# VectorE's product of rank and class ahead of the next step's first mask, in a kernel of linear attention and two feed-forward layers

## The chip, the core and the metric

The kernel runs on one core of a Trainium2 chip. The metric is the device time of one execution in microseconds (us). The kernel before took 776.17 us in the median of three runs.

## The reference

Three layers follow each other. The first is a linear attention with a decaying state, for 4 sequences, 8 heads, 768 positions and 48 channels:

```python
for t in range(S):
    cur = np.einsum('bhd,bhe->bhde', u[None] * kt, vt)
    y[:, :, t] = np.einsum('bhd,bhde->bhe', rt, state + cur)
    state = wt[:, :, :, None] * state + np.einsum('bhd,bhe->bhde', kt, vt)
```

The second sends each of the 3072 tokens (384 numbers each) to one of 8 experts, if its skip score is above zero; the third is a dense layer of 2048 inner channels:

```python
do_compute = x @ w_skip > 0
logits = xc @ w_gate
e_idx = np.argmax(logits, axis=1)
gate_w = probs[np.arange(len(xc)), e_idx]          # softmax of the logits
y[mask] = gate_w[mask, None] * (relu(xc[mask] @ w1[e]) @ w2[e])
out[do_compute] = xc + y
...
h = x @ w_in
return (h * np.clip(h + 3.0, 0.0, 6.0) / 6.0) @ w_out
```

## The kernel before

The order of the instructions on each engine is that of the code (`tc.manual_schedule()`); semaphores for the data are put in by the framework. Each engine works through its queue in order.

The first stage is the attention and the choice of the expert. A position of the loop `for i in range(-4, NST + 1)` (line 668) is called a step. `NST` is 24: chunk `c = i // 4` of 128 positions, sequence `b = i % 4`. In a step the engines work on several `i` at once:

- VectorE runs the decay of later steps: `state(i - 1)` (L569, `scan` L431, L573), `scan_end`, `scan_inv` and `scan_back` (L436, L439, L446). Then it masks the scores of the next step, in two halves: `masked(i + 1, 0)` and `masked(i + 1, 1)`, both L494. Behind them it adds up the output of the step in `x_out(i)` (L546).
- TensorE computes the next step's scores (`scores(i + 1)`, L490, two PSUM tiles `sc0` and `sc1`, one for each mask, written in turns), the step's output in `apply` (L524 to L534), the transposes and the diagonal of the next step in `k_xpose(i + 1)` (L504, L507, tile `kp`), the update of the state (L558, L560, tile `sl`) and the logits of the step before (L595, also in `sl`).
- GpSimd scales `r` and `k` (L456), multiplies them (L470), splits weights for the next stage (L276) and scatters the tokens to the experts' rows (`scatter`, L657).

Once in four steps the class of the tokens of a chunk is chosen. In steps 5, 9, 13, ... `gate_a` finds the class as a row of zeros and a one (`od`), and `gate_rank` lets TensorE count which row of the expert each token gets (`rnk`, L629 to L633). In steps 6, 10, 14, ... `gate_b` turns the counts into an index: the sum of `ex`, a small number on top, the reciprocal, the product `o1` of `rnk` and `od` (L645), its sum `si` (L648), and the new total of tokens in each class (L651 to L653). The last chunk is done in two halves behind the loop.

`rnk` and the tile of `k_xpose` have the same tag in a pool with one buffer:

```python
kp = ps_s.tile([128, 512], F32, tag="kp", name="kp")
...
rnk = ps_s.tile([128, 512], F32, tag="kp", name="rnk")[:, 0:nb * E1].rearrange(
```

so `k_xpose(i + 1)` can write it only when L645 has read `rnk`.

Behind the first stage come the experts (lines 852 to 885) and the dense layer (lines 982 to 999).

Of the kernel before, what the change touches and what calls it, by code (L numbers as in the profile page):

```python
# [8 lines left out]
F32 = mybir.dt.float32  # L9
# [5 lines left out]
ALU = mybir.AluOpType  # L15
AX = mybir.AxisListType

B, H, S, D = 4, 8, 768, 48
# [4 lines left out]
NCH = S // C  # L23
NST = NCH * B
# [3 lines left out]
E1 = E + 1  # L28
# [181 lines left out]
def rwkv_moe_kernel(ctx: ExitStack, tc: tile.TileContext, ch, vt, u, w9, wx, wm, out):  # L210
    nc = tc.nc
# [55 lines left out]
    def w_hi(e, q):  # L267
        t = wcur["raw", e, q]
        hi, lo = w_new(e % 2, q)
        nc.scalar.activation(out=hi, in_=t, func=ACTF.Copy)  # L270
        wcur[e, q] = (hi, lo)
# [73 lines left out]
    with tc.manual_schedule():  # L345
# [11 lines left out]
        with ExitStack() as p1:  # L357
# [5 lines left out]
            sm = p1.enter_context(tc.tile_pool(name="sm", bufs=2))  # L363
# [5 lines left out]
            def load_ch(i):  # L369
                t = chp.tile([PP, 1541], F32, tag="ch", name="ch")  # L370
                if i == 0:
                    nc.sync.dma_start(out=t[:, 1024:1541], in_=ch[i, :, 1024:1541])
                    nc.sync.dma_start(out=t[:, 0:1024], in_=ch[i, :, 0:1024])
                else:
                    nc.sync.dma_start(out=t, in_=ch[i])
                chb[i] = t
# [58 lines left out]
            def scan_end(i):  # L435
                nc.vector.tensor_scalar(out=pgp, in0=pw[i][1], scalar1=P_LO, scalar2=None, op0=ALU.max)  # L436

            def scan_inv(i):
                nc.vector.reciprocal(out=pw[i][0][:, 516:1032].rearrange("p (a b) -> p a b", a=PR)[:, :, 127],  # L439
                                     in_=pgp)  # L440
# [33 lines left out]
            def diag_v(i):  # L474
                dv = wk.tile([128, H, D], F32, tag="dv", name="dv")
                dg = dgw.pop(i)
                for h in range(H):
                    nc.scalar.activation(out=dv[:, h, :], in_=vb[i][:, h * D:h * D + D], func=ACTF.Copy,
                                         scale=dg[:, h:h + 1])
                dvw[i] = dv  # L480
# [117 lines left out]
            gw, rkw, siw = {}, {}, {}  # L598
# [25 lines left out]
            def gate_rank(c, b0, nb):  # L624
                od = gw[c, b0][1]
                rnk = ps_s.tile([128, 512], F32, tag="kp", name="rnk")[:, 0:nb * E1].rearrange(
                    "p (b e) -> p b e", b=nb)
                rkw[c, b0] = rnk
                nc.tensor.matmul(rnk, ones, cum[:, None, :].to_broadcast([128, nb, E1]), start=True, stop=False)  # L629
                nc.tensor.matmul(rnk, ones[0:1, :], erow[:, None, :].to_broadcast([1, nb, E1]), start=False, stop=False)  # L630
                nc.tensor.matmul(rnk, tri, od, start=False, stop=(nb == 1))
                for b in range(nb - 1):
                    nc.tensor.matmul(rnk[:, b + 1:nb, :], ones, od[:, b:b + 1, :].to_broadcast([128, nb - 1 - b, E1]),  # L633
                                     start=False, stop=(b == nb - 2))

            def gate_b(c, b0, nb):
                xt = xt4[c][:, b0:b0 + nb, :]
                rnk = rkw.pop((c, b0))
                ex, od = gw.pop((c, b0))
                s4 = s4p[:, 0:nb]  # L640
                nc.vector.tensor_reduce(out=s4, in_=ex, axis=AX.X, op=ALU.add)
                nc.vector.tensor_scalar(out=s4, in0=s4, scalar1=1e-9, scalar2=None, op0=ALU.add)
                nc.vector.reciprocal(out=xt[:, :, DM], in_=s4)
                o1 = sm.tile([128, B, E1], F32, tag="o1", name="o1")[:, 0:nb, :]
                nc.vector.tensor_tensor(out=o1, in0=rnk, in1=od, op=ALU.mult)  # L645
                si = sm.tile([128, B], I32, tag="si", name="si")[:, 0:nb]
                with nc.allow_low_precision(reason="one term of the sum is not zero, a whole number"):
                    nc.vector.tensor_reduce(out=si, in_=o1, axis=AX.X, op=ALU.add)  # L648
                siw[c, b0] = si
                sd = sm.tile([128, E1], F32, tag="sd", name="sd")  # L650
                nc.vector.tensor_reduce(out=sd, in_=od.rearrange("p b e -> p e b"), axis=AX.X, op=ALU.add)  # L651
                nc.vector.tensor_tensor(out=cumf, in0=cumf, in1=sd, op=ALU.add)
                nc.vector.tensor_copy(out=cum, in_=cumf)  # L653
# [11 lines left out]
            def ok(i):  # L665
                return 0 <= i < NST

            for i in range(-4, NST + 1):
                if i >= W0 + 2 and wq:
                    w_hi(*wq[0])  # L670
                if ok(i):
                    diag_v(i)
                if ok(i - 1):
                    state(i - 1)
                elif ok(i + 4):
                    scan(i + 4)
                if ok(i + 4):
                    scan_end(i + 4)
                    scan_inv(i + 4)
                    if i + 4 > 0:  # L680
                        scan_back(i + 4)
                if i == -4:
                    for a in (0, 2):
                        scan_back(0, a, a + 2)
                        scale(0, a, a + 2)
                    scale_rest(0)
                if i == -3:
                    scale(1)
                    scale_rest(1)
                if i == -3:  # L690
                    scores(0)
                    for g in range(2):
                        masked(0, g)
                    k_xpose(0)
                    warm1(WN)
                if ok(i + 3) and i + 3 >= 2:
                    scale(i + 3)
                    scale_rest(i + 3)
                if 7 <= i < NST - 1:
                    scatter(*divmod(i - 7, B))  # L700
                if i == NST - 1:
                    for b in range(B):
                        scatter(NCH - 2, b)
                if i < -2:
                    load_ch(i + 7)
                if ok(i + 6) and i + 6 > 4:
                    load_ch(i + 6)
                if i >= 0 and ok(i + 1):
                    scores(i + 1)
                    masked(i + 1, 0)  # L710
                if ok(i):
                    apply(i, 0)
                if ok(i - 1):
                    xpose(i - 1)
                if i >= W0 + 2 and wq:
                    w_lo(*wq.pop(0), nc.gpsimd)
                if i >= W0 and rq:
                    w_raw(*rq.pop(0))
                if i >= 5 and (i - 5) % 4 == 0 and i < NST:
                    gate_a((i - 5) // 4, 0, B)  # L720
                if i >= 6 and (i - 6) % 4 == 0 and i < NST:
                    gate_b((i - 6) // 4, 0, B)
                if i >= 0 and ok(i + 1):
                    masked(i + 1, 1)
                if ok(i):
                    apply(i, 1)
                    x_out(i)
                if i >= 0 and ok(i + 1):
                    k_xpose(i + 1)
                if ok(i):  # L730
                    state_mm(i)
                if -1 <= i < 1:
                    warm1(WN)
                if i == NST - 1:
                    logits(i - 2)
                    gate_a(NCH - 1, 0, 2)
                    logits(i - 1)
                elif ok(i - 1) and i < NST - 2:
                    logits(i - 1)
                if i >= 5 and (i - 5) % 4 == 0 and i < NST:  # L740
                    gate_rank((i - 5) // 4, 0, B)
                for e in range(2 * i - 4, 2 * i - 2) if 2 <= i < 6 else ():
                    xs0.append(nc.sync.dma_start(
                        out=xs[e * NT:e * NT + CAP, :].rearrange("(s p) x -> p s x", p=128),
                        in_=zrow[:, None, :].to_broadcast([128, CAP // 128, XR])))
                if ok(i + 5):
                    load_v(i + 5)
            gate_rank(NCH - 1, 0, 2)
            gate_b(NCH - 1, 0, 2)
            logits(NST - 1)  # L750
            for b in range(2):
                scatter(NCH - 1, b)
            warm1(4, "sc0")
            for f in (gate_a, gate_rank, gate_b):
                f(NCH - 1, 2, 2)
            for b in range(2, B):
                scatter(NCH - 1, b)
# [10 lines left out]
        op = p2.enter_context(tc.tile_pool(name="op", bufs=2))  # L768
# [120 lines left out]
        op = fast.enter_context(tc.tile_pool(name="yp", bufs=2))  # L889
# [174 lines left out]
```

## Time and profile before

| | us |
|---|---|
| median of 3 runs | 776.17 |
| lowest and highest run | 771.25 and 777.05 |
| the profiled execution | 781.31 |
| its span, first to last instruction | 779.6 |
| TensorE busy | 745.7 (96%) |
| VectorE busy | 498.4 (64%) |
| ScalarE busy | 346.7 (44%) |
| GpSimd busy | 219.1 (28%) |

The times of rows are from the start of the span of the profiled execution. PE is TensorE's matmuls, PEld its loading of weights, DVE VectorE, ACT ScalarE, POOL GpSimd, SP SyncE with its queue of transfers. In a timeline a row has its start, the time it takes (for several instructions that are shown as one, from the first to the last), engine, line, operation, output and inputs, the count, and in brackets how long the engine stood idle before it and what released it. A row may begin before the one ahead of it has ended, since neighbours overlap.

### The profile page before, as it was taken

The page shows a single profiled execution, that of the slowest core. Times are in us where ns is not written, and L with a number is a line of the kernel's source. Part 1 is how long each engine was busy: PE and PEld are TensorE (multiplying, and loading weights), DVE is VectorE, ACT ScalarE, POOL GpSimd, SP SyncE. Part 2 cuts the span into 40 slices and gives each one's busy share as a digit, 9 for nine tenths or more (in the row PEclk, how much of TensorE's full clock was granted, in tenths as well). Part 3 has the DMA queues.
Part 4 walks back from the last instruction along what each step waited for, and adds up shares of the span by engine and source line. Part 5 has one row for each costly group of instructions (what it writes and reads, how often), then busy time and mean ns, then how long its engine had stood idle before and what let it go on. Part 6 is the DMA issues. An engine that isn't in the chain of part 4 may idle for free.

```text
span 779.6 us, 14596 instructions
## 1 busy us (share of the span) xinstructions
PE 745.7 (96%) x5653; PEld 613.5 (79%) x5653; DVE 498.4 (64%) x974; ACT 346.7 (44%) x796; POOL 219.1 (28%) x192
## 2 busy tenths in 40 slices
PE   8799999998999999798999999999999999999995
PEld 4587787784999999786777888888888888788884
DVE  8879986763899999965887444454545444433331
ACT  2366664552766566525554333333233333333331
POOL 4646987853253535431443000000000000000000
PEclk9599996999999999999999999999999999999998
DMA  8689887523877788114231220031022001001001
GB/s 219 193 240 269 243 230 205 152 71 98 287 261 257 260 257 287 52 41 148 84 97 44 76 65 25 33 86 47 12 77 77 24 14 40 1 0 42 0 1 45
DMA packets 40590, 90.84 MB, mean 117 GB/s; under 512 B 5442, under 2 KB 19552, under 8 KB 40512
## 3 DMA queue, kind: packets, MB, share of 16 engines
q1 hardware_dynamic: 37952, 85.14, 35.7%
q0 software_dynamic: 2560, 4.69, 1.7%
q8 instruction: 46, 0.75, 0.4%
q14 instruction: 32, 0.26, 0.1%
HBM read 72.51 MB, written 20.53 MB: 119 GB/s over the span
## 4 chain that ended last, share of the span: by engine, by line
PE 52%; DVE 20%; issue 3%; DMA 2%; ACT 2%; SPq 1%; POOL 0%; DVEq 0%; POOLq 0%; ACTq 0%
PE f L774 8%; PE f L777 8%; PE f L775 8%; PE acc L937 8%; PE acc L939 7%; PE acc L936 7%; DVE wlo L276 5%; DVE wlo L327 2%; DVE hl L815 2%; DVE a L304 2%; DVE a L307 2%; DVE f L922 1%; DVE gl L924 1%; ACT gh L923 1%; DVE a L302 1%
## 5 line engine op out<-in xcount | busy, mean ns | idle before, releaser
L922 DVE SCALAR_TENSOR_TENSOR f<-t,f 128x512 f32<-128x512 f32 x96 | 66.6, 694 | 128.4 <-ACT t L921 128.4
L921 ACT ACTIVATE t<-f,three 128x512 f32<-128x512 f32 x96 | 66.1, 689 | 158.3 <-PE f L777 158.3
L937 PE MATMUL acc<-gh,wlo 128*128 128x512 f32 x288 | 115.0, 399 | 2.1 <-DVE wlo L327 1.9
L936 PE MATMUL acc<-gh,whi 128*128 128x512 f32 x288 | 115.7, 402 | 0.0
L774 PE MATMUL f<-bh,whi 128*128 128x512 f32 x288 | 114.4, 397 | 0.6 <-ACT bh L909 0.6
L775 PE MATMUL f<-bh,wlo 128*128 128x512 f32 x288 | 114.1, 396 | 0.0
L924 DVE TENSOR_TENSOR gl<-f,gh 128x512 fp32r<-128x512 f32 x96 | 66.4, 692 | 63.9 <-ACT gh L923 63.9
L923 ACT ACTIVATE gh<-f 128x512 fp32r<-128x512 f32 x96 | 57.5, 599 | 99.6 <-DVE f L922 99.6
L939 PE MATMUL acc<-gl,whi 128*128 128x512 f32 x288 | 84.0, 396 | 0.0
L777 PE MATMUL f<-bl,whi 128*128 128x512 f32 x288 | 83.0, 396 | 0.0
L937 PEld LDWEIGHTS acc<-gh,wlo 128*128 128x128 f32 x288 | 54.3, 188 | 17.5 <-DVE wlo L327 5.5
L276 DVE TENSOR_TENSOR wlo<-raw,whi 128x768 fp32r<-128x768 f32 x52 | 66.0, 1269 | 0.0
L314 POOL TENSOR_TENSOR lf<-lf,ab 128x384 f32<-128x384 f32 x32 | 32.5, 1014 | 118.0 <-DVE ab L308 101.3
L774 PEld LDWEIGHTS f<-bh,whi 128*128 128x128 f32 x288 | 54.2, 188 | 13.9 <-ACT bh L909 0.8
L270 ACT ACTIVATE whi<-raw 128x768 fp32r<-128x768 f32 x64 | 54.2, 847 | 24.7 <-DMA raw<-in_wx_dram 24.5
L939 PEld LDWEIGHTS acc<-gl,whi 128*128 128x128 f32 x288 | 54.2, 188 | 13.3
L777 PEld LDWEIGHTS f<-bl,whi 128*128 128x128 f32 x288 | 54.2, 188 | 13.3
L775 PEld LDWEIGHTS f<-bh,wlo 128*128 128x128 f32 x288 | 54.3, 188 | 13.1
L936 PEld LDWEIGHTS acc<-gh,whi 128*128 128x128 f32 x288 | 54.3, 189 | 11.8
L456 POOL TENSOR_TENSOR rkt<-ch,p 112x1024 f32<-112x1024 f32 x22 | 47.9, 2178 | 37.0 <-PE x L529 23.6
L774 PE MATMUL f<-xh,whi 128*128 128x256 f32 x192 | 50.4, 291 | 6.1 <-DVE hl L815 5.3
L775 PE MATMUL f<-xh,wlo 128*128 128x256 f32 x192 | 48.9, 283 | 0.0
(149 smaller groups left out, 1436.3 us busy)
## 6 DMA issues: line engine op xcount, KB each, us to landing
raw<-in_wx_dram SPq DMA_DIRECT2D x64, 384.0 KB, 4.8
ch<-in_ch_dram SPq DMA_DIRECT2D x23, 674.2 KB, 5.5
draw<-in_wm_dram SPq DMA_DIRECT2D x32, 384.0 KB, 5.0
cw<-in_ch_dram SPq DMA_DIRECT2D x24, 226.2 KB, 2.7
v<-in_vt_dram SPq DMA_DIRECT2D x24, 192.0 KB, 3.2
xo<-xt SPq DMA_DIRECT2D x24, 192.0 KB, 3.0
xb<-xo SPq DMA_DIRECT2D x24, 192.0 KB, 3.8
out_dram<-y SPq DMA_DIRECT2D x17, 256.0 KB, 2.2
```

What stands on the lines that cost most here:

```text
L270: nc.scalar.activation(out=hi, in_=t, func=ACTF.Copy)
L276: (eng or nc.vector).tensor_tensor(out=lo, in0=t, in1=hi.bitcast(F32), op=ALU.subtract)
L774: nc.tensor.matmul(o, wh, xh, start=(i == 0), stop=False)
L775: nc.tensor.matmul(o, wl, xh, start=False, stop=False)
L777: nc.tensor.matmul(o, wh, xl, start=False, stop=(i == len(ws) - 1))
L921: nc.scalar.activation(out=t, in_=p, func=ACTF.Relu, bias=three)
L922: nc.vector.scalar_tensor_tensor(out=p, in0=t, scalar=6.0, in1=p, op0=ALU.min, op1=ALU.mult)
L923: nc.scalar.activation(out=hi, in_=p, func=ACTF.Copy)
L924: nc.vector.tensor_tensor(out=lo, in0=p, in1=hi.bitcast(F32), op=ALU.subtract)
L936: nc.tensor.matmul(acc[k][m], wh[:, os_[m]:os_[m] + 128], hi, start=(j == 0), stop=False)
L937: nc.tensor.matmul(acc[k][m], wl[:, os_[m]:os_[m] + 128], hi, start=False, stop=False)
L939: nc.tensor.matmul(acc[k][m], wh[:, os_[m]:os_[m] + 128], lo, start=False, stop=(j == 15))
```

## The change

The product of `rnk` and `od` moves out of `gate_b` into a function of its own, `gate_o`. In the loop it is called in the same step as `gate_b`, but ahead of `scores(i + 1)` and `masked(i + 1, 0)`. Behind the loop it is called directly in front of `gate_b`.

```diff
+            def gate_o(c, b0, nb):
+                ex, od = gw.pop((c, b0))
+                o1 = sm.tile([128, B, E1], F32, tag="o1", name="o1")[:, 0:nb, :]
+                nc.vector.tensor_tensor(out=o1, in0=rkw.pop((c, b0)), in1=od, op=ALU.mult)
+                gw[c, b0] = ex, od, o1
+
             def gate_b(c, b0, nb):
                 xt = xt4[c][:, b0:b0 + nb, :]
-                rnk = rkw.pop((c, b0))
-                ex, od = gw.pop((c, b0))
+                ex, od, o1 = gw.pop((c, b0))
                 s4 = s4p[:, 0:nb]
...
                 nc.vector.reciprocal(out=xt[:, :, DM], in_=s4)
-                o1 = sm.tile([128, B, E1], F32, tag="o1", name="o1")[:, 0:nb, :]
-                nc.vector.tensor_tensor(out=o1, in0=rnk, in1=od, op=ALU.mult)
                 si = sm.tile([128, B], I32, tag="si", name="si")[:, 0:nb]
...
+                if i >= 6 and (i - 6) % 4 == 0 and i < NST:
+                    gate_o((i - 6) // 4, 0, B)
                 if i >= 0 and ok(i + 1):
                     scores(i + 1)
                     masked(i + 1, 0)
...
             gate_rank(NCH - 1, 0, 2)
+            gate_o(NCH - 1, 0, 2)
             gate_b(NCH - 1, 0, 2)
...
-            for f in (gate_a, gate_rank, gate_b):
+            for f in (gate_a, gate_rank, gate_o, gate_b):
```

On VectorE's queue step 6 of the loop reads so before (`sc_970` and `sc_971` are the two halves of the scores, `cb` the tile with small results, `o_1007` the product):

```order
L446 SCALAR_TENSOR_TENSOR p<-ch,p,cb 112x127 x3
L494 TENSOR_TENSOR at<-sc_970,mask 128x4x128 [waits PE_49]
L641 TENSOR_REDUCE cb<-ex 128x4 [waits DVE_49,Activation_49]
L642 TENSOR_SCALAR cb<-cb 128x4 [waits DVE_49]
L643 RECIPROCAL xt<-cb 128x4 [waits DVE_49]
L645 TENSOR_TENSOR o_1007<-rnk,od 128x36
L648 TENSOR_REDUCE si<-o_1007 128x4 [waits DVE_49]
L651 TENSOR_REDUCE sd<-od 128x9
L652 TENSOR_TENSOR cb<-cb,sd 128x9 [waits DVE_49]
L653 CAST cum<-cb 128x9 [waits DVE_49]
L494 TENSOR_TENSOR at<-sc_971,mask 128x4x128 [waits PE_49]
```

and so now (the lines behind the new function are 4 to 6 higher):

```order
L446 SCALAR_TENSOR_TENSOR p<-ch,p,cb 112x127 x3
L640 TENSOR_TENSOR o_969<-rnk,od 128x36 [waits PE_49]
L494 TENSOR_TENSOR at<-sc_972,mask 128x4x128 [waits PE_49]
L647 TENSOR_REDUCE cb<-ex 128x4 [waits DVE_49,Activation_49]
L648 TENSOR_SCALAR cb<-cb 128x4 [waits DVE_49]
L649 RECIPROCAL xt<-cb 128x4 [waits DVE_49]
L652 TENSOR_REDUCE si<-o_969 128x4
L655 TENSOR_REDUCE sd<-od 128x9
L656 TENSOR_TENSOR cb<-cb,sd 128x9 [waits DVE_49]
L657 CAST cum<-cb 128x9 [waits DVE_49]
L494 TENSOR_TENSOR at<-sc_973,mask 128x4x128 [waits PE_49]
```

The product has moved from behind the reciprocal to a place ahead of the first mask and has a wait for TensorE of its own; the sum `si` has lost its wait for VectorE.

In the first gate behind the loop, on VectorE too, before (`od` is the row of the class, `ex` the exponentials):

```order
L620 TENSOR_TENSOR od<-cd_154,cb 128x18 [waits DVE_49]
L641 TENSOR_REDUCE cb<-ex 128x2 [waits DVE_49,Activation_49]
L642 TENSOR_SCALAR cb<-cb 128x2 [waits DVE_49]
L643 RECIPROCAL xt<-cb 128x2 [waits DVE_49]
L645 TENSOR_TENSOR o_3075<-rnk,od 128x18 [waits PE_49]
```

and now:

```order
L620 TENSOR_TENSOR od<-cd_154,cb 128x18 [waits DVE_49]
L640 TENSOR_TENSOR o_3072<-rnk,od 128x18 [waits DVE_49,PE_49]
L647 TENSOR_REDUCE cb<-ex 128x2 [waits Activation_49]
L648 TENSOR_SCALAR cb<-cb 128x2 [waits DVE_49]
L649 RECIPROCAL xt<-cb 128x2 [waits DVE_49]
```

Here the product moves in front of the sum of `ex`, with its wait for TensorE's rank. The queues of the other engines keep their order.

## Rows read from the trace of the kernel before

**Rows 1.** TensorE's waits, 40 to 190 us: who waited for whom, total, times, longest.

```profile
PE kp L504 <- DVE o L645: 4.6, 4, 1.2
```

**Rows 2.** Timeline of VectorE in step 6: start, duration, instruction, idle before it.

```profile
64.49 0.67 DVE L494 TENSOR_TENSOR at<-sc,mask 128x512 f32<-128x512 f32 x1
...
65.50 0.18 DVE L643 RECIPROCAL xt<-cb 128x4 f32<-128x4 f32 x1
65.60 0.16 DVE L645 TENSOR_TENSOR o<-rnk,od 128x36 f32<-128x36 f32 x1
65.79 0.19 DVE L648 TENSOR_REDUCE si<-o 128x4 int32<-128x36 f32 x1
...
66.43 0.68 DVE L494 TENSOR_TENSOR at<-sc,mask 128x512 f32<-128x512 f32 x1
...
67.91 0.37 DVE L569 TENSOR_TENSOR cb<-sl,st 112x192 f32<-112x192 f32 x1 [0.33 <-PE sl L595]
```

**Rows 3.** Timeline of TensorE in the same step.

```profile
64.35 0.39 PE L534 MATMUL x<-v,at 128*64 128x48 f32 x8
...
65.90 0.57 PE L504 MATMUL kp<-ident,rkt 112*128 112x112 f32 x4 [1.16 <-DVE o L645]
...
67.79 1.16 PE L490 MATMUL sc<-rkt 48*128 48x128 f32 x16
```

**Rows 4.** Timeline of VectorE: starts of L569, once in a step.

```profile
60.60 0.35 DVE L569 TENSOR_TENSOR cb<-sl,st 112x192 f32<-112x192 f32 x1
...
74.02 0.37 DVE L569 TENSOR_TENSOR cb<-sl,st 112x192 f32<-112x192 f32 x1 [0.49 <-PE sl L595]
...
86.68 0.35 DVE L569 TENSOR_TENSOR cb<-sl,st 112x192 f32<-112x192 f32 x1
...
93.98 0.37 DVE L569 TENSOR_TENSOR cb<-sl,st 112x192 f32<-112x192 f32 x1 [0.33 <-PE sl L595]
...
101.65 0.37 DVE L569 TENSOR_TENSOR cb<-sl,st 112x192 f32<-112x192 f32 x1 [1.29 <-PE sl L595]
...
121.63 0.37 DVE L569 TENSOR_TENSOR cb<-sl,st 112x192 f32<-112x192 f32 x1 [0.35 <-PE sl L595]
...
132.58 0.37 DVE L569 TENSOR_TENSOR cb<-sl,st 112x192 f32<-112x192 f32 x1 [2.77 <-PE sl L595]
...
141.36 0.37 DVE L569 TENSOR_TENSOR cb<-sl,st 112x192 f32<-112x192 f32 x1 [1.30 <-PE sl L595]
...
155.21 0.37 DVE L569 TENSOR_TENSOR cb<-sl,st 112x192 f32<-112x192 f32 x1 [0.33 <-PE sl L595]
...
162.20 0.37 DVE L569 TENSOR_TENSOR cb<-sl,st 112x192 f32<-112x192 f32 x1 [0.62 <-PE sl L595]
```

**Rows 5.** Stretches: length, busy time (instructions) by engine, TensorE's clock, DMA share, GB/s.

```profile
62.00:94.00 32.00, 29.69 (x586) 24.74 (x586) 29.02 (x82) 19.40 (x66) 24.66 (x18) 1.00 0.88 260
94.00:97.50 3.50, 3.50 (x26) 2.32 (x28) 3.30 (x8) 3.11 (x12) 3.32 (x3) 0.51 0.77 204
97.50:121.40 23.90, 22.75 (x462) 19.18 (x458) 20.47 (x55) 14.79 (x50) 21.34 (x17) 1.00 0.83 230
121.40:138.40 17.00, 17.00 (x173) 13.38 (x169) 10.48 (x23) 7.89 (x27) 10.21 (x9) 0.50 0.65 197
138.40:155.50 17.10, 15.95 (x323) 13.59 (x324) 13.70 (x40) 10.40 (x33) 15.61 (x10) 1.00 0.50 147
155.50:158.90 3.40, 3.40 (x30) 2.22 (x28) 3.20 (x9) 2.78 (x11) 3.15 (x3) 0.50 0.46 149
158.90:180.00 21.10, 21.10 (x432) 17.68 (x429) 10.38 (x29) 12.28 (x45) 12.03 (x12) 1.00 0.19 69
```

**Rows 6.** GpSimd's timeline, and the DMA issue at 88.03 (size, us to landing).

```profile
84.56 2.18 POOL L456 TENSOR_TENSOR rkt<-ch,p 112x1024 f32<-112x1024 f32 x1
...
90.99 2.17 POOL L456 TENSOR_TENSOR rkt<-ch,p 112x1024 f32<-112x1024 f32 x1
...
ch<-in_ch_dram SPq DMA_DIRECT2D x1, 674.2 KB, 5.2
```

## Prediction

> **What bounds the kernel now.** I read the waits by engine first, then the two timelines of one step of the chunk loop, then the starts of one VectorE line over the whole loop, then the granted clock stretch by stretch. The change touches only the first stage (to about 190 us of 779.6), so all of its gain or loss is made there; the rest of the span moves along behind it.
>
> In the table of waits TensorE waits for VectorE's product `o` four times, 4.6 us in all, 1.2 us at the longest [rows 1]. The two timelines show how [rows 2, 3]. In step i = 6 (and 10, 14, 18, called gate steps here) TensorE ends `apply` at 64.35 + 0.39 = 64.74 and wants to start `k_xpose`, whose tile has the tag `kp`, as `rnk` has; there is one buffer. Its last reader is the product of L645. VectorE starts that at 65.60 only, because it stands behind the first mask (64.49) and the sum, the offset and the reciprocal of `ex`. So TensorE stands from 64.74 to 65.90, which the row prices at 1.16 us.
>
> Who waits for TensorE then? L569 of the next step, which needs `sl`: it stands idle 0.33 us before 67.91, up to the end of L595 [rows 2]. In the steps between, it waits for the same line too (0.49 us before 74.02 [rows 4]), so there TensorE sets the pace, and what it lost in the gate step isn't caught up. Taken from start to start of L569 [rows 4], the gate step takes 67.91 - 60.60 = 7.31, the next one 74.02 - 67.91 = 6.11, and the four steps of a chunk 86.68 - 60.60 = 26.08 us.
>
> The clock carries more than this. TensorE is granted full clock to 94 us, though the first stall (64.74) lies in there; then half of it (1.2 of 2.4 GHz) for three stretches [rows 5]. The first follows the stall of step 10, which ended at about 92 us, and the one before 138.4 us and the last follow the stalls of steps 14 and 18 in the same way, some 2 us behind them. In front of each the engine did just what rows 3 show: it stood (4.6 us in four parts, so all about alike) and then ran the short matmuls of `k_xpose` and `logits`. No other place of the chunk loop between 62 and 180 us has a fall. What they cost is read from rows 4. The step from 93.98 took 7.67 us, 1.56 over the 6.11 of an ordinary one. The steps from 121.63 and 132.58 took 10.95 and 8.78, 4.84 and 2.67 over. The step from 155.21 took 6.99; it makes no transposes any more (the last chunk has no state to write), which an ordinary one does at 0.57 us [rows 3], so it is 6.99 - (6.11 - 0.57) = 1.45 over. Sum: 10.5 us.
>
> The profiled execution took 781.31 us, 5.1 us above the median of 776.17. Without falls it would be 781.31 - 10.5 = 770.8, and the lowest of the three runs is 771.25: I read that one as a run with hardly a fall, and the median as one with about half the falls of the profile.
>
> Of the same stall four times, three brought the clock down and one didn't. The Trainium skill, "TensorE: Matmul & The Clock Gate", section "What's actually happening", says that what watches the engine runs freely and is not started afresh with a kernel. By that rule one kernel has runs with more and with fewer falls; the trace agrees (three of four), and the spread of 771.25 to 777.05 fits.
>
> **The change, part by part.** Nothing is added or removed: seven products move, five of them in front of `masked(i + 1, 0)`, two at the very end in front of the sum of `ex`. No DMA and no instruction of another engine moves.
>
> *The product itself.* It would start where the mask stands now, 64.49, since `rnk` is written by matmuls that stand in TensorE's queue in front of the score matmuls for which the mask waits anyhow; so it can add no wait of its own there. At 0.16 us it ends at 64.65. Before, the transposes came 65.90 - (65.60 + 0.16) = 0.14 us behind its end, so now at 64.79: 1.11 us sooner, and nearly all of the wait is gone, since `apply` ends at 64.74.
>
> *The first mask* starts later by the product's slot. Two neighbours without a wait stand 0.10 us apart (65.50 to 65.60), so 0.10. Where it stood, the product and the sum behind it took 0.10 + 0.19 (65.50 to 65.79); with the product gone the sum follows the reciprocal by 0.10. So the second mask starts 0.09 us sooner, at 66.34, and ends at 67.02. Behind the first mask are queued the gate's sums, the second mask and `x_out`; only the first mask is later, and its reader is the next step's `apply`, over 3 us away.
>
> *Where TensorE's wait goes.* Its work up to the score matmuls comes 1.11 us sooner, so the scores would start at 67.79 - 1.11 = 66.68. The second of them writes the bank that the second mask reads, and that mask ends at 67.02. So TensorE stands again, for about 0.35 us, and goes on at about 67.1 where it had 67.79 + 0.07: 0.76 us sooner. This is the term that I take. Its bounds: 0.42 if only VectorE's idle time and slot count (0.33 + 0.09), 1.11 if the new wait is nothing.
>
> *Who passes it on.* VectorE's L569 no longer waits in the gate step; from the next step on TensorE sets the pace and hands on its 0.76. Four gate steps stall: 4 x 0.76 = 3.0 us (1.7 to 4.4). The fifth, i = 22, has no transposes and no such wait in rows 1: nothing.
>
> *GpSimd.* It runs one step in 90.99 - 84.56 = 6.43 us without a pause [rows 6], and a chunk would now take 26.08 - 0.76 = 25.3, so it would fall behind by some 0.4 us a chunk. What it frees late is the buffer of `ch`. The load issued at 88.03 lands 5.2 us later [rows 6], and its scan stands behind L569 at 101.65, in undisturbed steps some 7 us behind the landing. So the cover holds, and I cost it at nothing; without it the chunks of steps 10 to 19 would stay at GpSimd's pace (a rival below).
>
> *The last two gates.* Behind the loop the product stands in front of the sum, the offset and the reciprocal, which before could run while TensorE counted `rnk`. It is needed for `si` either way, so the loss is at most those three, 0.44 us from the first mask's end to the product (65.16 to 65.60 [rows 2]), and 0.9 us for both gates; the other bound is nothing. I take nothing, since the count is a few short matmuls, and keep 0.9 for the range.
>
> *The clock.* With the stall at 0.35 us in place of 1.16, what TensorE does around it is like the step in front of it (i = 5, 9), which has the rank's short matmuls and in no row brings a fall. I take all three falls as gone: 10.5 us of the profile, 5.4 of the median.
>
> **Sum**: 781.31 - 10.5 - 3.0 = 767.8 us; from the lowest run 771.25 - 3.0 = 768.2.
>
> **Rivals.**
> *The falls stay* (the shorter stall is enough, or another thing brings them). Then the median keeps its 5.4 us: 776.17 - 3.0 = 773.2. For it: the stall of step 6 brought none, so the stall alone does not decide. Against: all three stand behind such a stall. The skill's page on the clock gate, section "HAM oscillation", would have the engine throttled only by gaps longer than any that it has here; by that rule the falls aren't this wait's doing and this rival holds. The three falls of rows 5 speak against the rule.
> *Another engine keeps the pace*: GpSimd at 6.43, or the second mask held longer than reckoned. The falls go, the 3.0 us don't come: 770.8.
> *Slower*: the wait in front of the second score matmul comes at a worse moment for the clock. A long fall costs 7.5 us (4.84 + 2.67), a short one 1.5. From 767.8, two long and one short give 784.3, over 1% above the median; with fewer it is no slowdown. In the profile one of three was long.
>
> **How the numbers follow.** Forecast 0.68, falls stay 0.14, another pace 0.13, slower 0.05. The forecast's own range is 765.5 (4.4 us per chunk term, and a cheaper start) to 770. The range that leaves out no more than 2 in 10 takes in the second and third case: 765.5 to 773.5. One per cent is about what a measurement can tell from no change: 768.4. Three quarters of the forecast lie below it: faster 0.50, same 0.46, slower 0.04. Predicted: 767.8.
>
> **What would show it.** In the changed profile: no wait of `kp` for the product; a wait of the score matmuls for the mask of about 0.35 us instead; gate steps of about 6.9 us and chunks of 25.3 between starts of L569; full clock from 62 to 180 us. It is wrong if half clock still stands behind gate steps, or if chunks without a fall still take 26 us.

## The result, and the profile after

The changed kernel took 764.95 us in the median of four runs (763.07 to 766.15), against 774.37 us before: a ratio of 0.9878, with a 95% interval of 0.9829 to 0.9926. It is faster, as forecast, but 0.55 us below the range of 765.5 to 773.5. Two later measurements on other chips gave 772.12 us (0.9926, 0.9882 to 0.9969) and 768.60 us (0.9873, 0.9832 to 0.9914). The 774.37 us have one run more than the 776.17 of before the change: a fourth, of 772.56 us, taken beside the changed kernel. The profiled execution took 764.39 us.

The wait of [rows 1] is gone. This is the whole table of TensorE's waits after the change, 40 to 150 us, with its columns (gaps under 0.15 us are not listed):

```profile
engine line waited for: us in total, times, longest us
PE kp L504 <- PE x L534: 0.2, 1, 0.2
```

The gate step on VectorE, the timeline that answers to [rows 2] (L640 is the product, L494 the masks, L652 the sum):

```profile
60.32 0.17 DVE L640 TENSOR_TENSOR o<-rnk,od 128x36 f32<-128x36 f32 x1
60.41 0.68 DVE L494 TENSOR_TENSOR at<-sc,mask 128x512 f32<-128x512 f32 x1
...
61.42 0.18 DVE L649 RECIPROCAL xt<-cb 128x4 f32<-128x4 f32 x1
61.52 0.16 DVE L652 TENSOR_REDUCE si<-o 128x4 int32<-128x36 f32 x1
...
62.13 0.68 DVE L494 TENSOR_TENSOR at<-sc,mask 128x512 f32<-128x512 f32 x1
...
63.20 0.35 DVE L569 TENSOR_TENSOR cb<-sl,st 112x192 f32<-112x192 f32 x1
...
69.10 0.37 DVE L569 TENSOR_TENSOR cb<-sl,st 112x192 f32<-112x192 f32 x1 [0.29 <-PE sl L595]
```

The product holds the mask for 0.09 us (60.32 to 60.41), the sum follows the reciprocal by 0.10, and L569 no longer stands idle at the end of the gate step. TensorE in the same step, which answers to [rows 3]:

```profile
60.18 0.39 PE L534 MATMUL x<-v,at 128*64 128x48 f32 x8
60.54 0.60 PE L504 MATMUL kp<-ident,rkt 112*128 112x112 f32 x4
...
62.45 1.57 PE L490 MATMUL sc<-rkt 48*128 48x128 f32 x16
```

The transposes follow `apply` at once. The 16 score matmuls last 1.57 us in place of 1.16: the 0.41 us between is the new wait for the second mask, which ends at 62.13 + 0.68 = 62.81. It lies between two of the 16, so it has no line in the table of waits; where the mask is moved out of the way (e7_sums_last, below), they last 1.16 us again.

The stretches that answer to [rows 5] (length, busy time by engine, granted clock, DMA share, GB/s):

```profile
62.00:94.00 32.00, 32.00 (x615) 26.60 (x611) 29.96 (x78) 21.85 (x75) 27.87 (x21) 1.00 0.91 254
94.00:97.50 3.50, 3.50 (x59) 2.73 (x56) 3.01 (x8) 3.48 (x14) 3.32 (x4) 1.00 1.02 257
97.50:121.40 23.90, 23.74 (x457) 19.82 (x455) 22.19 (x59) 16.73 (x57) 23.32 (x17) 1.00 0.90 254
121.40:138.40 17.00, 17.00 (x344) 14.37 (x343) 15.78 (x48) 11.44 (x39) 16.42 (x14) 1.00 0.78 233
138.40:155.50 17.10, 17.10 (x334) 14.44 (x334) 11.60 (x29) 11.84 (x43) 13.95 (x12) 1.00 0.24 80
...
177.00:184.00 7.00, 6.42 (x33) 6.30 (x31) 2.84 (x7) 3.03 (x7) 0.00 (x0) 0.51 1.00 370
```

The loop runs at full clock throughout. Full clock "from 62 to 180 us", as forecast, came to 177 us only: the experts' first matmuls run at half clock, where those of before didn't. That the change has to do with this isn't shown.

To see where the time went, I cut each profiled execution at four events: L569 of step 6, L569 of step 20, the first matmul of the experts, and the first of the dense layer. The last part includes what lies around the span.

| profile | up to step 6 | steps 6 to 20 | to the experts | experts | dense layer | sum |
|---|---|---|---|---|---|---|
| before | 60.60 | 101.60 | 32.53 | 160.51 | 426.07 | 781.31 |
| after | 56.43 | 88.27 | 33.00 | 161.87 | 424.82 | 764.39 |

Of the 16.92 us between the two, 13.33 lie in the loop, where 13.5 (10.5 + 3.0) were forecast. The other large part, 4.17 us, lies ahead of step 6, where the change alters nothing. The three parts behind the loop together are 0.58 us longer (0.47 + 1.36 - 1.25).

### The profile page after: what moved, and what is told of

It reads as the page before. It is cut to its first block, busy times and chain, and to the rows that moved or that the text cites. A ratio compares the mean times of both kernels' runs of the same rounds, so it can differ in the third digit from the quotient of the medians.

```text
span 762.6 us, 14593 instructions
## 1 busy us (share of the span) xinstructions
PE 735.4 (96%) x5653; PEld 607.0 (80%) x5653; DVE 497.6 (65%) x974; ACT 346.7 (45%) x796; POOL 218.7 (29%) x192
## 4 chain that ended last, share of the span: by engine, by line
PE 65%; DVE 25%; DMA 4%; issue 2%; ACT 2%; SPq 0%; POOL 0%; DVEq 0%; ACTq 0%
PE acc L944 8%; PE f L781 8%; PE acc L946 8%; PE acc L943 8%; PE f L784 8%; PE f L782 8%; DVE wlo L276 7%; PE sc L490 3%; PE x L534 3%; PE x L529 3%; DVE hl L822 2%; PE x L524 2%; DVE wlo L327 2%; DVE a L304 2%; DVE a L307 2%
## 5 line engine op out<-in xcount | busy, mean ns | idle before, releaser
L314 POOL TENSOR_TENSOR lf<-lf,ab 128x384 f32<-128x384 f32 x32 | 32.5, 1015 | 119.2 <-DVE ab L308 100.8
```

## The experiments

The theory: the product's wait cost pace in the loop (3 us) and half clock behind gate steps; what else differs is chance. The rivals: the half clock has another cause; the change acts on the start or the tail too; or it helps by VectorE's order, not by TensorE's wait.

**The kernel before once more.** No edit.

> The kernel before once more, to see how one kernel's executions differ. If half clock is what spreads its times, the profiles of one kernel show different stretches at half clock, in the first 40 us as well as behind gate steps, the start of L569 in step 6 lies anywhere from 56 to 61 us, and the time is 767 to 782 us with the length of the half clock. If only the falls behind gate steps vary, L569 of step 6 starts within 0.5 us of 60.6 in each.

774.99 us (0.9964, 0.9932 to 0.9997, against the same program run beside it; so an interval that misses 1 by a few ten-thousandths shows nothing). In its profile step 6 begins at 61.18 us, and all four gate steps bring a fall: the loop takes 98.68 us. The ten runs lie between 769.87 and 782.58. Each run on record also has its mean granted clock: over the 96 runs of this kernel behind the first measurement the time falls as that clock rises (correlation -0.85). So half clock goes with the spread of the times, but this profile didn't show another start; a later one did (55.63, below).

**The rank in a place of its own.** The product stays where it was.

```diff
-                rnk = ps_s.tile([128, 512], F32, tag="kp", name="rnk")[:, 0:nb * E1].rearrange(
-                    "p (b e) -> p b e", b=nb)
+                rnk = cb[:, 320:320 + nb * E1].rearrange("p (b e) -> p b e", b=nb)
```

> The rank goes into free columns of the tile cb in place of the tag kp; the product stays where it was before. If the wait of k_xpose for the product is what costs, it goes here too: no wait of L504 for the product, gate steps of 6.9 us, no half clock behind gate steps, and 763 to 768 us like the change (0.988 of before). If the moved product helps in another way (VectorE's slot, the sum without its wait), this stays at 772 to 777 us.

767.99 us, 0.9894 (0.984 to 0.9948). TensorE has no wait over 45 to 150 us, gate steps take 6.90 us, the loop 88.79, all at full clock:

```profile
61.40 0.36 DVE L569 TENSOR_TENSOR cb<-sl,st 112x192 f32<-112x192 f32 x1
...
68.30 0.35 DVE L569 TENSOR_TENSOR cb<-sl,st 112x192 f32<-112x192 f32 x1
```

```profile
45.00:150.00 105.00, 104.59 (x2011) 87.09 (x2012) 96.18 (x252) 71.85 (x243) 88.99 (x65) 1.00 0.87 246
```

So the wait for `kp` is the cause. What the order adds on VectorE is the 0.13 us between 6.90 and the 6.77 of the changed kernel.

**The wait filled with matmuls, which missed its aim.** 12 matmuls of ones into free columns of `cb` ahead of `k_xpose` in gate steps; everything else as before.

```diff
+                if i >= 6 and (i - 6) % 4 == 0 and i < NST:
+                    for _ in range(12):
+                        nc.tensor.matmul(cb[:, 320:512], ones, ones[:, 0:96, None].to_broadcast([128, 96, 2]),
+                                         start=True, stop=True)
                 if i >= 0 and ok(i + 1):
                     k_xpose(i + 1)
```

> The order of before, with 12 matmuls of ones by ones on 192 columns (results unused) put in front of k_xpose in gate steps, so that TensorE is busy during most of its wait for the product. If the falls come from the stall, there is no half clock between 45 and 180 us, while the gate step keeps its 7.3 us and a chunk its 26.1: 3.0 us over the change, 767 to 769 us. If the falls have another cause, half clock stays behind gate steps and the time is that of before, 772 to 777 us.

778.31 us, 1.0032 (0.9989 to 1.0074). The timeline of TensorE in step 6 shows why it isn't what I had meant:

```profile
63.63 1.15 PE L730 MATMUL cb<-ones 128*128 128x192 bf16 x12 [1.83 <-DVE cum L653]
64.62 0.55 PE L504 MATMUL kp<-ident,rkt 112*128 112x112 f32 x4
```

The fill itself waits 1.83 us for VectorE's work in the same tile, so it stands behind a longer stall and makes the gate step 8.94 us long. It still tells something: no gate step of this profile brings a fall, though the stall is longer than that of [rows 3]. The mean granted clock agrees over all runs: its median is 0.984 in these ten and 0.976 in the nineteen of before beside them. Stretch by stretch around three of its gate steps:

```profile
60.00:68.00 8.00, 6.17 (x118) 5.50 (x115) 5.74 (x18) 3.25 (x12) 4.05 (x3) 1.00 0.83 234
92.00:98.00 6.00, 6.00 (x117) 5.04 (x117) 3.84 (x10) 4.41 (x15) 4.13 (x3) 1.00 0.62 183
120.00:126.00 6.00, 6.00 (x122) 5.05 (x119) 3.84 (x11) 4.45 (x15) 4.14 (x3) 1.00 0.69 196
```

A stall with a row of wide matmuls behind it did not bring the clock down in these four gate steps; a shorter one between `apply` and the thin matmuls of `k_xpose` and `logits` did, in 9 of the 16 gate steps of the four profiles with the old order (before, e0_before, e6_warm_before, e12_before).

**The wait filled, second try.** The fill goes into the free buffer of `x`, for which it need not wait.

```diff
+                if i >= 6 and (i - 6) % 4 == 0 and i < NST:
+                    t = ps_x.tile([128, DM], F32, tag="x", name="fill")
+                    for _ in range(6):
+                        nc.tensor.matmul(t.rearrange("p (a b) -> p a b", a=3), ones,
+                                         ones[:, None, :].to_broadcast([128, 3, 128]), start=True, stop=True)
```

> What e2_fill was to be: the fill goes into the free buffer of the tile x, 6 matmuls of 384 columns that wait for nothing, so they lie inside TensorE's wait for the product (1.1 of 1.16 us). If the falls come from thin work around the stall, none stands behind a gate step, while gate steps keep 7.3 and chunks 26.1 us: 3.0 us over the change on the same chip. If the falls don't hang on this place: as many as before (8 of 12 gate steps in the three profiles of that kernel's loop) and the time of before.

770.79 us, 0.9941 (0.9908 to 0.9975). Here the fill lies in the wait, the transposes start where they did, and the steps keep their old length (65.33 to 71.44 is 6.11, and the gate step ahead of it 7.31):

```profile
62.09 1.15 PE L731 MATMUL fill<-ones 128*128 128x384 bf16 x6
63.33 0.57 PE L504 MATMUL kp<-ident,rkt 112*128 112x112 f32 x4
...
65.33 0.37 DVE L569 TENSOR_TENSOR cb<-sl,st 112x192 f32<-112x192 f32 x1 [0.33 <-PE sl L595]
...
71.44 0.37 DVE L569 TENSOR_TENSOR cb<-sl,st 112x192 f32<-112x192 f32 x1 [0.49 <-PE sl L595]
```

```profile
45.00:150.00 105.00, 104.68 (x1976) 85.80 (x1973) 94.21 (x249) 70.64 (x242) 88.51 (x65) 1.00 0.84 240
```

No fall in this profile. The median of the mean granted clock is 0.985 in these ten runs and 0.975 in the nineteen of before beside them. The loop takes 91.08 us: this is the old order without half clock, and the change's 88.27 are the 2.8 us of pace below it. The falls are the rest: the four profiles with the old order have loops of 101.60, 98.68, 94.09 and 94.24 us, 6.1 us over 91.08 in the mean.

**The product the other way**, behind the second mask, with its sum `si`, in the kernel before (here `gate_o` holds both; behind the loop it also stands behind `gate_b`):

```diff
                 if i >= 0 and ok(i + 1):
                     masked(i + 1, 1)
+                if i >= 6 and (i - 6) % 4 == 0 and i < NST:
+                    gate_o((i - 6) // 4, 0, B)
...
```

> The product and its sum go the other way, behind the second mask, so TensorE waits about 1.25 us longer in each gate step (2.4 us in all). By the pace alone that is 4 x 1.25 = 5.0 us over before, 779 us; the stall being longer, each gate step should bring a fall, at 1.5 to 7.5 us each, where before had about half of that: 780 to 795 us. If the clock does not hang on the stall: 779 us with as much half clock as before.

788.86 us, 1.0185 (1.0123 to 1.0247). TensorE's wait in the gate step has doubled, and each of the four brings half clock (three of the stretches here):

```profile
63.54 0.57 PE L504 MATMUL kp<-ident,rkt 112*128 112x112 f32 x4 [2.30 <-DVE o L640]
```

```profile
58.00:64.50 6.50, 4.20 (x79) 3.23 (x75) 5.81 (x19) 1.82 (x6) 2.24 (x2) 1.00 0.92 292
64.50:71.30 6.80, 6.80 (x80) 5.50 (x78) 4.83 (x11) 3.45 (x13) 2.47 (x2) 0.50 0.76 210
95.20:102.00 6.80, 6.80 (x78) 5.50 (x75) 4.96 (x11) 4.06 (x14) 4.11 (x3) 0.50 0.75 211
125.90:132.70 6.80, 6.80 (x68) 5.17 (x65) 4.96 (x11) 3.82 (x15) 3.96 (x3) 0.50 0.78 214
```

The loop takes 106.58 us. More wait, more time and more half clock (median of the mean granted clock 0.9645, before 0.976): the theory holds in this direction too.

**The product half way**, behind the first mask; the edit is to the changed kernel:

```diff
-                if i >= 6 and (i - 6) % 4 == 0 and i < NST:
-                    gate_o((i - 6) // 4, 0, B)
                 if i >= 0 and ok(i + 1):
                     scores(i + 1)
                     masked(i + 1, 0)
+                if i >= 6 and (i - 6) % 4 == 0 and i < NST:
+                    gate_o((i - 6) // 4, 0, B)
```

> The product behind the first mask, ahead of the sum of ex. TensorE then waits for it until about 0.6 us later than in the change: a stall of 0.5 in place of 1.16 us, and the scores come when the second mask has just been done, so the pace is almost that of the change (0.6 of 0.76 us a gate step). If a stall of 0.5 is short enough for the clock: 764 to 767 us. If it brings falls as before: 768 to 775 us.

769.72 us, 0.9887 (0.9854 to 0.9921). TensorE waits 0.66 us, the gate step takes 6.80 us and the next one 6.11, the loop 89.11 at full clock:

```profile
59.83 0.57 PE L504 MATMUL kp<-ident,rkt 112*128 112x112 f32 x4 [0.66 <-DVE cb L647]
```

The time lies in the 768 to 775 us that were said for the case with falls, but on a chip where before ran at 778.54; the loop decides. A stall a little over half as long brought no fall in the four gate steps of this profile; with 9 in 16 before, that could still be chance in about 4 of 100 profiles, if each gate step fell by itself. The mean granted clock over all ten runs, 0.980 in the median against 0.974 of before beside them, speaks for no falls.

**The start filled.** In both kernels 24 matmuls of ones in place of 5 at the end of step 0, where TensorE waits for GpSimd (4.42 us in the profile of before, up to 24.73):

```diff
                 if -1 <= i < 1:
-                    warm1(WN)
+                    warm1(WN if i else 24)
```

With the order of before:

> The kernel before with 24 in place of 5 matmuls of ones at the end of step 0, which fill TensorE's wait for the first work of GpSimd (20.3 to 24.7 us of the profile of before). If the start's half clock is a matter of that stall, the first 40 us run at full clock, L569 of step 6 starts at 56 us or sooner, and the time is 767 to 775 us: the falls behind gate steps stay. If the start is not what differs between executions, the time is that of before.

773.49 us, 0.9948 (0.9907 to 0.9989). With the change:

> The same 24 matmuls in the changed kernel. If the start's half clock is an independent part, it goes here too: full clock from 16 to 170 us, 1 to 4 us off the changed kernel's 764.95, so 761 to 764 us, and 0.5 to 1.3% under the kernel e6_warm_before by pace (3 us) and falls. If the change had acted on the start, both would start alike and the gap to e6_warm_before would be only 3 us.

767.13 us, 0.9847 (0.9787 to 0.9908). Both start at full clock; the first profiles of before and after the change did not. The stretch of 15 to 40 us in the profiles of before, after, e6_warm_before and e5_warm_after, in this order, each in a fence:

```profile
15.00:40.00 25.00, 20.58 (x235) 15.48 (x233) 19.91 (x45) 9.43 (x38) 15.91 (x11) 0.66 0.66 190
```

```profile
15.00:40.00 25.00, 21.93 (x318) 16.33 (x317) 23.64 (x54) 12.46 (x49) 17.16 (x12) 0.86 0.80 226
```

```profile
15.00:40.00 25.00, 24.63 (x371) 17.75 (x371) 23.98 (x55) 13.60 (x52) 17.23 (x13) 1.00 0.77 225
```

```profile
15.00:40.00 25.00, 24.52 (x359) 17.45 (x359) 24.05 (x55) 13.24 (x51) 17.10 (x12) 1.00 0.77 225
```

Step 6 begins at 54.84 and 55.28 us there, against 60.60 and 56.43. Over all 17 profiles of these experiments step 6 goes with the half clock that begins between 22 and 28 us. Where it lasts 17 us (before, e0_before, e1_own_tile), step 6 begins at 60.60 to 61.40; with 13.7 us (e10_after_again) at 60.85; with 3.4 to 6.9 us at 56.43 to 58.16; and where none begins there, at 54.84 to 56.32. All five profiles with the start filled are of the last kind, and two of the twelve without. With like starts the two orders still differ by 6.36 us in the median, so the change works without the start. Of that, 2.8 us are pace; the other 3.6 are not read from a trace, but the one fall in e6_warm_before's loop cost 94.09 - 91.08 = 3.0. The absolute 761 to 764 us that I had expected for e5_warm_after didn't come: the kernel before ran at 778.54 us beside it, over 4 us above the 774.37 of the first measurement.

**The change once more**, without an edit:

> The changed kernel once more, on the chip of e9_fill_x, e8 and e11. If the start is luck, its L569 of step 6 lies anywhere from 55 to 61 us in the profile, and all of its distance to the first profile's (56.43) shows in the time, while the chunk loop from step 6 to step 20 takes 88.3 us as there. If the change had shortened the start, step 6 begins near 56.4 again.

772.12 us, 0.9926 (0.9882 to 0.9969), on a chip where before ran at 776.78. The loop takes 88.28 us, but step 6 begins at 60.85 and the part up to the experts takes 36.65 in place of 33.00 us. So e9_fill_x, which was to be 3.0 us over the change on this chip, came out 1.3 us under it: the pace of 2.8 us is read from the loops, and the times of the two don't show it. Their runs cover each other (769.50 to 775.01 and 766.59 to 775.93), and step 6 began 2.83 us sooner in the profile of e9_fill_x. The longer tail asked for both kernels on one chip:

> The kernel before on one chip with e13_after, to read its tail (from L569 of step 20 to the experts' first matmul) there. If the longer tail of e10_after_again (36.7 against 33.0 us, with gaps between TensorE's matmuls in step 23) belongs to the chip or the execution, it is as long here. If the faster loop causes it, it is 32.5 us here and 36 to 37 in e13_after. The loop from step 6 to 20 takes 91.1 us and 1.5 to 7.5 more for each fall behind a gate step.

> The changed kernel beside e12_before. The loop from step 6 to 20 takes 88.3 us again, with no half clock in it. By the loop alone it is 2.8 us faster and by the falls another 2 to 10 in each execution, so a ratio of 0.986 to 0.993; if the tail gives 3 to 4 us back, 0.990 to 0.998.

Before: 776.31 us (0.9981, 0.9955 to 1.0007, against itself). After: 768.60 us, 0.9873 (0.9832 to 0.9914). The profiles, cut as above, with e9_fill_x as the old order without falls:

| profile | up to step 6 | steps 6 to 20 | to the experts | experts | dense layer | sum |
|---|---|---|---|---|---|---|
| e0_before | 61.18 | 98.68 | 32.54 | 161.56 | 426.45 | 780.41 |
| e12_before | 55.63 | 94.24 | 36.20 | 160.27 | 426.92 | 773.26 |
| e10_after_again | 60.85 | 88.28 | 36.65 | 160.99 | 426.78 | 773.55 |
| e13_after | 57.35 | 88.29 | 35.76 | 160.83 | 425.42 | 767.65 |
| e9_fill_x | 58.02 | 91.08 | 35.46 | 161.18 | 426.78 | 772.52 |

The tail, from step 20 to the experts, is 36.20 us before and 35.76 after on that chip: it belongs to the chip or the execution, and the faster loop doesn't cause the 3 us. The loop takes 88.3 us in each of three profiles of the change. The start lies anywhere from 55.6 to 61.2 us in the kernel before and from 56.4 to 60.9 in the changed one.

**Going on from the change.** The gate's sums behind the second mask, so that the scores wait for nothing:

```diff
-                if i >= 6 and (i - 6) % 4 == 0 and i < NST:
-                    gate_b((i - 6) // 4, 0, B)
                 if i >= 0 and ok(i + 1):
                     masked(i + 1, 1)
+                if i >= 6 and (i - 6) % 4 == 0 and i < NST:
+                    gate_b((i - 6) // 4, 0, B)
```

> The changed kernel, with the gate's sums moved behind the second mask as well. The score matmuls then find both masks done and TensorE loses the 0.4 us that it still waits there. VectorE sets the pace of the gate step (6.8 us), TensorE of the next two: 0.25 us a chunk, 1.0 us in all, so 763 to 766 us. If TensorE's wait there was not in the way: no difference to the change.

769.01 us, 0.9884 (0.9825 to 0.9942). The scores take 1.16 us again, and the step behind the gate 5.53 us in place of 5.90; the loop takes 87.52 us. The 763 to 766 us didn't come; the unaltered change was not run on this chip, so only the loop shows the gain, 0.75 us. With the start filled as well:

> The changed kernel with the gate's sums behind the second mask (e7) and 24 matmuls at the end of step 0 (e5). Both gains together: 1.2 us from the loop (87.5 in place of 88.3 us from step 6 to 20) and the start at full clock (step 6 from about 55 us): 1 to 4 us under e10_after_again. If the start's luck is as often good without the fill, only the 1 us.

767.41 us, 0.988 (0.9809 to 0.9952), where e10_after_again stood at 772.12 (the intervals of the ratios overlap); loop 87.05, step 6 from 56.32. With 8 more matmuls ahead of the experts:

```diff
-        warm(24)
+        warm(32)
```

> e8_sums_last_warm with 32 in place of 24 matmuls in front of the experts' first transposes, where the changed kernel and e5, e3, e7 had a stretch at half clock (160 to 184 us). If that stretch comes from TensorE's wait for the first tokens, it is gone and the time is 1 to 3 us under e8. If it starts earlier, in the last steps of the loop, no difference.

767.07 us, 0.9897 (0.9822 to 0.9973): no difference to e8_sums_last_warm that this can tell. A stretch at half clock still came in the last steps of the loop (from 153.9 us). Then e8's kernel once more:

> The kernel of e8_sums_last_warm beside e13_after in more rounds: 87.0 us from step 6 to 20, and a start of 55 to 56.5 us in each execution in place of 55 to 61: 1 to 4 us under e13_after.

766.65 us, 0.984 (0.9806 to 0.9874), beside 768.60 for the change: 0.25% less, and the intervals overlap. The loop's 1.25 us are read from the profile (87.04 against 88.29); a gain of the whole over the change isn't shown beyond the measurement.

## Why the prediction was right, and where it was wrong

*The stall and its cause*: right. The wait for `kp` is gone, and it goes in e1_own_tile without moving the product.

*The terms of the pace*: right. The 0.07 us that it gives the second score matmul stands in no row (in the trace that starts 0.01 us behind the first); the term came out all the same. The mask is held 0.09 us where 0.10 was reckoned; the new wait of the scores is 0.41 where 0.35 was; a chunk takes 81.75 - 56.43 = 25.32 us where 25.3 was said. Its 0.76 us come as 0.54 in the gate step (7.31 to 6.77, where 6.9 was said) and 0.21 in the next. Over four gate steps it is 91.08 - 88.27 = 2.8 us where 3.0 was reckoned. Two starts of L569, one chunk apart:

```profile
56.43 0.35 DVE L569 TENSOR_TENSOR cb<-sl,st 112x192 f32<-112x192 f32 x1
...
81.75 0.35 DVE L569 TENSOR_TENSOR cb<-sl,st 112x192 f32<-112x192 f32 x1
```

*GpSimd at nothing*: right. It now takes 25.8 to 26.0 us for a chunk in the middle of the loop, more than the 25.3 of the pace, and still no row of TensorE, VectorE or ScalarE waits for it between 56 and 165 us.

*The last two gates at nothing*: too low by 0.27 us on VectorE, within the 0.9 kept for the range. VectorE now stands 0.28 us for the rank in each, as in the first:

```profile
164.44 0.18 DVE L640 TENSOR_TENSOR o<-rnk,od 128x18 f32<-128x18 f32 x1 [0.28 <-PE rnk L633]
```

From the start of `od` to that of `si` the two gates take 1.26 and 1.13 us, before 1.15 and 0.97. Whether this reaches the time isn't shown: the tail is 0.47 us longer than before's in the first two profiles, and 0.44 shorter in e13_after than in e12_before.

*The falls behind gate steps*: right. They come from the stall with the thin matmuls behind it: none in the three profiles of the change, none where the rank has its own place (e1_own_tile) or the wait is filled (e9_fill_x), four of four with the wait doubled (e4_late). Their size of 10.5 us is that of one profile; over four it is 6.1.

*Two rules of the Trainium skill.* The Trainium skill, "TensorE: Matmul & The Clock Gate", section "What's actually happening", says that what watches the engine runs freely. The prediction took from this that one kernel has executions with more and with fewer falls, and the runs agree: 3, 4, 1 and 1 falls in four profiles of the old order. By the rule of the Trainium skill, same page, section "HAM oscillation", these gaps would be too short; it does not hold here, since falls stand behind gaps of 1.16 us, and the rival built on it is out.

*What failed* is the step from the one profile to the time: in "781.31 - 10.5 - 3.0" everything outside the loop keeps the value that it had in that execution, the start among it, at 60.60 us, because the change doesn't touch it. But the start's half clock comes and goes like that of the gate steps: step 6 began at 60.60, 61.18 and 55.63 us in three profiles of before, and at 56.43, 60.85 and 57.35 in three of the change. The profile that I summed from had one of the late ones, and the first profile after an early one, 4.17 us sooner. 767.8 less 4.17 is 763.6; that execution took 764.39. The low end of the range had "a cheaper start" in it, but without a row for it and at 0.9 us (767.8 less the 1.4 of the upper bound of the pace is 766.4, and the range began at 765.5). With the 5 us between early and late starts it would have been 762.8, and 764.95 lies within.

The profiled execution alone shows its start; of the other three runs only the mean granted clock is known. It is 0.983 to 0.988 in the four, and 0.974 to 0.986 in the 16 runs of the two later measurements, so all four were on the good side of what is chance. Taken from median to median, 8.4 us were forecast (5.4 + 3.0) and 9.42 measured; the other 1.8 us of the 2.85 between 767.8 and 764.95 are the fourth run of before, which moved its median from 776.17 to 774.37.

That the 770.8 us without falls came out next to the lowest run's 771.25 looked like a check and was none: that run has no trace, and a run can as well have an early start and some falls, as e12_before had (55.63 us and one fall).

The later medians, 772.12 and 768.60 us, lie inside the range. They come from chips on which before took 776.78 and 779.07, so they don't bear the forecast of the time out; they show that between executions and chips more moves than the 2.8 us of pace.

*The chances*: faster by over 1% had 0.50, same 0.46. The three ratios are 0.9878, 0.9926 and 0.9873, two beyond the line of one per cent and one within it; the interval of each holds that line, so none of them settles it.

## What to carry to other kernels

Where a tile shares its one buffer with another tile, the engine that writes it next waits for the last reader, here 1.16 us in each gate step: put the reader ahead of whatever doesn't feed it, and price the engine that waits, not the one that reads. Where a short stall stands next to thin matmuls, look at the granted clock some microseconds behind it, since the fall can cost more than the stall (10.5 us against 4.6 in the profile of before). And before summing from one profile, look at the clock in the parts that the edit does not touch, and profile the same kernel once more; what is chance there belongs in the range.

## What was not expected of the hardware

A stall of 1.83 us with a row of wide matmuls behind it brought no half clock in four gate steps (e2_fill), while one of 1.16 us with thin matmuls behind it did in 9 of 16, and one of 0.66 in none of four (e3_behind_mask). On three of the chips TensorE also stood between matmuls of the loop's last steps without anything that the profile shows, in both kernels. In e12_before's timeline, for one:

```profile
166.51 0.24 PE L529 MATMUL x<-sbd,rkt 112*64 112x96 f32 x1 [0.29 <-issue]
...
167.26 0.32 PE L534 MATMUL x<-v,at 128*64 128x48 f32 x4 [0.38 <-issue]
...
168.67 0.20 PE L534 MATMUL x<-v,at 128*64 128x48 f32 x1 [1.08 <-issue]
```

Half clock follows in e12_before (169.6 to 179.9 us). In e9_fill_x the gaps bring none up to the experts, and its tail is long all the same, so it is not the half clock that makes it so: profiles with these gaps have tails of 35.5 to 38.2 us, in both orders, and those without 32.5 to 33.7. What holds TensorE in them stays open.
